# One Trainium2 core, attention into a snake MLP: transposes of two batches reordered, one MLP pass with four PSUM slots and no output matmuls

## The chip, the cores and the metric

The kernel runs on one core of one Trainium2 chip. The metric is device time in microseconds of one execution, given as the median of several runs. The program is written with an explicit order: each engine (TensorE is PE, its weight loads are PEld, VectorE is DVE, ScalarE is ACT, GpSimd is POOL, SyncE is SP) executes its instructions in the order in which the kernel's Python code emits them, and semaphores order the engines against each other.

## The reference

There are 4 batches of 8 heads with 768 positions and head size 64. The sequence is cut into chunks of 32 queries; each chunk attends to 8 memory keys, 16 keys to the left, its own 32 and 8 to the right. The attention output, laid out as 3072 tokens of 512 numbers, goes through an MLP with a "snake" activation:

```
scores = scale * q_c @ k_full.T          # k_full: 8 memory keys + local context
a      = softmax(scores)
out[:, :, chunk] = a @ v_full
x = out as (4*768, 8*64)
h = x @ w_in                             # 512 -> 2048
s = sin(alpha * h)
g = h + s * s / (alpha + 1e-9)
y = g @ w_out                            # 2048 -> 512
```

Inputs and output are float32; the kernel computes its matmuls in bfloat16 and accumulates in float32.

## The kernel before, in words

**One batch at a time, four times over.** For each batch an attention stage produces `xT`, the attention output transposed (512 features on 4x128 partitions, 768 tokens). Then a `layer` runs the first MLP matmul over 16 feature tiles `ft`: `first` issues 8 matmuls of 384 columns (L454) into a two-bank PSUM slot, ACT takes the sine (L474), one of ACT, DVE or POOL squares it (letters A, V, P of a string; L478 for ACT, L481 for the other two), and DVE's `finish` (L484) makes `gT[ft]` and frees the slot. The finish of `ft` is emitted in the next iteration, or two later when POOL squares. The number of slots in the ring `h` says how far PE may run ahead of the finishes.

**The output matmuls are a feed.** `second(i, gT)` is a generator of 6x16 matmuls of 512 columns (L497) for batch i; sub-block s copies its bank to `o_sb` on DVE if s is even (L508) and on ACT if odd (L510), and SP sends it out (L511). `feed.take(n)` puts the next n of these matmuls into PE's order at that point. So batch i's output matmuls are spread through the attention stage of batch i+1 (the tuple `shares` gives how many a step takes, half before the values, half after) and through its `layer` (`to_feed`).

**Batch 0.** `attention_first` works by head pairs. `turns(hp)` transposes keys and queries on PE (L232) into the two banks of ring `t`; `put_k` copies the keys' middle on ACT (L239) and their two edges on DVE (L245), `put_q` copies the queries on DVE (L251). `sc(hp)` issues two units of scores (mask bias L323, products L331), each followed by one exponential on ACT (L338). Then come eight units of values: `pv` is 8 matmuls (L350), followed by a reciprocal and a multiply on DVE (L356, L357); `x` is 4 transposes (L367) and an ACT copy into `xT` (L370). `warm(1)` is one matmul of 512 columns on zeros (L318), whose result is used by nobody; it takes a bank from ring `one`, as `x` does. `put_memv(0)` (L188) writes batch 0's memory values into the values tile on DVE. `ahead` issues the first half of the MLP's first three feature tiles.

**Batch 1.** POOL's `pair_up` (L220) lays two heads side by side, `turn` transposes them on PE (L229), and `put_k`/`put_q` copy as above. `put_memk(1)` (L198) writes the memory keys into the key tile on DVE.

**Batches 2 and 3.** `load_rows(b)` loads keys and queries by POOL's DMA queue into `kst` and `qst`. `cross(b)` lets SP transpose them by DMA, first eight key tiles (L159), then six query tiles (L161). It is emitted in `layer(b-1)` at `ft == 2`. SP's queue is in order too: before `cross(2)` stand the output DMAs of attention stage 1 and the eight DMAs of `send_memv(2)` (L195).

**Attention of batches 1 to 3** has 8 blocks of 96 queries. Step s issues `scores` of block s (L265, then three exponentials L278), and `values` of block s-2 (L291, reciprocal L297, multiply L298 on DVE) and `turn_x` of block s-3 (L308, DVE copy L311). The activation table of ACT is changed before and after the exponentials.

POOL's queue at the start issues, in this order: keys and queries of batch 0 (8 DMAs), memory values, V of batch 0 (two edges and eight parts), the first MLP weight (5), the second (2), keys and queries of batch 1.

Of the kernel before, what the change touches and what calls it, by code (L numbers as in the profile page):

```python
# [9 lines left out]
P = 128  # L10
# [3 lines left out]
BF = mybir.dt.bfloat16  # L14
F32 = mybir.dt.float32
ACTF = mybir.ActivationFunctionType
# [26 lines left out]
def kernel(  # L43
# [12 lines left out]
    nc = tc.nc  # L56
    B, H, S, D = q.shape
# [4 lines left out]
    HP = H // 2  # L62
# [11 lines left out]
    blk = ctx.enter_context(tc.tile_pool(name="blk", bufs=3))  # L74
# [35 lines left out]
    kTs = [consts.tile([P, HP, KW], BF, name=f"kT{i}") for i in range(2)]  # L110
# [9 lines left out]
    memk_st = consts.tile([P, 2, H * D], BF, name="memk_st")  # L120
# [42 lines left out]
    def load_qk(b, bufs, h0, h1):  # L163
        for src, dst in ((k, bufs[0]), (q, bufs[1])):
            nc.gpsimd.dma_start(
                dst[:, h0:h1].rearrange("p h r d -> p h (r d)"),
                src[b, h0:h1].rearrange("h (p r) d -> p h (r d)", p=P),
            )

    def load_v(b, parts=((0, H),)):  # L170
        vw = vws[b % 2][:].rearrange("p h j c -> p (h j) c")
        vf = v[b].rearrange("h (j t) d -> t (h j) d", t=QW)
        n = H * NJ
        if len(parts) > 1:
# [41 lines left out]


    def pair_up(src, hp):
        pr = blk.tile([P, 6, 2, D], BF, name="pr")
        nc.gpsimd.tensor_copy(  # L220
            pr[:].rearrange("p r e d -> p e r d"), src[:, 2 * hp:2 * hp + 2]
        )
        return pr

    def turn(src, hp, pr):
        t = packed(single("t"), 6, P)
        for r in range(6):
            if pr is not None:
                nc.tensor.transpose(t[:, r, :], pr[:, r].rearrange("p e d -> p (e d)"), ident[:])  # L229
            else:  # L230
                for e in range(2):
                    nc.tensor.transpose(  # L232
                        t[64 * e:64 * e + 64, r, :], src[:, 2 * hp + e, r, :], ident[:]
                    )
        return t

    def put_k(b, hp, t):
        kT = kTs[b % 2]
        nc.scalar.copy(  # L239
            kT[:, hp, 72:72 + 7 * 104].rearrange("p (s c) -> p s c", c=104)[:, :, 0:96]  # L240
            .rearrange("p s (a r) -> p s a r", r=6),
            t[:, :, 8:120].rearrange("p r (s a) -> p s a r", a=16),
        )
        for t0, c0 in ((0, 16), (120, 800)):
            nc.vector.tensor_copy(  # L245
                kT[:, hp, c0:c0 + 48].rearrange("p (a r) -> p a r", r=6),
                t[:, :, t0:t0 + 8].rearrange("p r a -> p a r"),
            )

    def put_q(b, hp, t, scalar=False):  # L250
        (nc.scalar.copy if scalar else nc.vector.tensor_copy)(  # L251
            qTs[b % 2][:, hp, :].rearrange("p (a r) -> p a r", r=6),
            t.rearrange("p r a -> p a r"),
        )
# [60 lines left out]
    def warm(n):  # L315
        z = single()
        for _ in range(n):
            nc.tensor.matmul(z, idle[:, 0:P], idle[:])  # L318
# [55 lines left out]
    def attention_first(kq, alphas, ahead):  # L374
        xT = xp.tile([P, KT, S], BF, name="xT")
        pt, xb = {}, {}

        def turns(hp):
            put_k(0, hp, turn(kq[0], hp, None))
            put_q(0, hp, turn(kq[1], hp, None))  # L380

        def sc(hp):
            for half in range(2):
                pt[hp, half] = unit_scores(hp, half)

# [12 lines left out]
        warm(2)  # L398
        turns(1)
        sc(0)  # L400
        alphas()
        sc(1)
        turns(2)
        sc(2)
        turns(3)
        put_memv(0, nc.vector, 0, H)
        sc(3)
        nc.scalar.preload_act_table(ACTF.Sin)
        send_memv(1)
        plan(big=rings["t"][0:1] + rings["big"])  # L410
        units = [(hp, half) for hp in range(HP - 1) for half in range(2)]
        pv(0, 0)
        for n in range(1, len(units)):
            pv(*units[n])
            warm(1)
            x(*units[n - 1])
            warm(1)
        pv(3, 0)
        x(2, 1)
        pv(3, 1)  # L420
        x(3, 0)
        ahead(0, 0, xT)
        ahead(1, 0, xT)
        x(3, 1)
        ahead(2, 0, xT)
        return xT
# [89 lines left out]
    kq = alloc_qk()  # L516
# [12 lines left out]
    for hp in range(1, HP):  # L529
        load_qk(0, kq, 2 * hp, 2 * hp + 2)  # L530
    nc.gpsimd.dma_start(memv_st[64:72].rearrange("n b h d -> n (b h) d"),
                        mem_v.rearrange("b h n d -> n (b h) d"))
    load_v(0, [(2 * hp, 2 * hp + 2) for hp in range(HP)])
    for kT in kTs:
        nc.vector.memset(kT[:, :, 0:16], 0.0)
        nc.vector.memset(kT[:, :, 848:856], 0.0)
# [34 lines left out]

    feed = Feed()
    xT = attention_first(kq, alphas, ahead)
    for c in range(2):
        load_w_out(c)
    kq1 = alloc_qk()
    load_qk(1, kq1, 0, H)

# [4 lines left out]
    def layer(i, xT, squares, begin, to_feed):  # L583
        gT = gTs[i % 2]
        pend = []
        fed = 0
        for ft in range(FT):
            begin(ft)
            square = squares[ft % len(squares)]
            squared, fin = first(ft, xT, gT, square, begun.pop(ft, None))  # L590
            want = to_feed * (ft + 1) // FT
            feed.take(want - fed)
            fed = want
            for due, f in [p for p in pend if p[0] <= ft]:
                f()
            pend = [p for p in pend if p[0] > ft]
            squared()
            pend.append((ft + (2 if square == "P" else 1), fin))
        for due, f in pend:
            f()  # L600
        feed.add(second(i, gT), NSUB * FT)

    def begin_0(ft):
        if ft == 3:
            plan(h=[6] + rings["big"])
        if ft == 9:
            load_v(1)

    layer(0, xT, "VPAPAAVPAAVAVPAA", begin_0, 0)
    last4 = rings["h"]  # L610
    plan(one=(last4[0], last4[0] + 1), t=(last4[1], last4[1] + 1), big=last4[1:])
    for bb in range(2):
        nc.gpsimd.dma_start(memk_st[64:72].rearrange("n b (h d) -> n b h d", d=D)[:, bb],
                            mem_k[2 + bb].rearrange("h n d -> n h d"))
    put_memk(1)
    feed.take(8)
    prs = [pair_up(kq1[n % 2], n // 2) for n in range(3)]
    for pc in range(2 * HP):
        t = turn(None, pc // 2, prs[pc])
        (put_k if pc % 2 == 0 else put_q)(1, pc // 2, t)  # L620
        if pc + 3 < 2 * HP:
            prs.append(pair_up(kq1[(pc + 3) % 2], (pc + 3) // 2))
        feed.take(2)
        if pc == 2 * HP - 2:
            nc.scalar.preload_act_table(ACTF.Exp)
    feed.take(4)
    load_rows(2)
    xT = attention(1, feed, (4, 4, 4, 3, 3, 3, 3, 3, 3, 3, 3), 2, 0)
    load_v(2)
    send_memv(2)  # L630

    for i in range(1, B):
        last = i == B - 1

        def begin(ft, i=i):
            if ft == 2 and i + 1 < B:
                cross(i + 1)

        plan(h=rings["big"])
        layer(i, xT, "AAAV", begin, feed.left() - (0 if last else 16))  # L640
        if not last:
            if i + 2 < B:
                load_rows(i + 2)
            plan(big=rings["h"])
            nc.scalar.preload_act_table(ACTF.Exp)
            xT = attention(i + 1, feed, (10, 8, 4, 4, 3, 3, 3, 3, 4, 4, 4), 2, 5 if i == B - 2 else 0)
            if i + 2 < B:
                load_v(i + 2)
                send_memv(i + 2)
# [31 lines left out]
```

## Time and profile before

| what | value |
|---|---|
| median of 5 runs | 232.55 us (230.77 to 235.52) |
| the profiled execution's own time | 233.45 us |
| span of the profile, first to last instruction | 231.7 us |
| PE busy | 216.7 us, 94% of the span |
| DVE, ACT, POOL busy | 135.9, 153.2, 81.8 us |
| largest groups on PE | L497 101.9 us x384, L454 91.9 us x512 |

The page counts a matmul busy from its issue to its modelled end, and matmuls overlap in the pipeline; so 94% is not 94% of peak, and the time that one matmul costs the queue is read from start to start: 0.2165 us for 512 columns and 0.163 us for 384 columns in the dense stages. A bracket in a timeline row says how long the engine was idle before the row and what ended that. What lies outside the span is 1.75 us.

The stages lie so in the profile: batch 0's transposes, scores and values 5.5 to 33, its MLP pass 33 to 55.5, batch 1's transposes 57.7 to 65.7, its attention 65.7 to 81.5, its MLP pass 81.5 to 107, attention of batch 2 107 to 125, its MLP pass to 156, batch 3 to 206, the last output matmuls to the end.

### The profile page before, as it was taken

Reading aid. Unit: us, or ns where it says so; the run is one execution under the profiler, and the core shown is the slowest. Engines: PE = TensorE matmul, PEld = TensorE weight load, DVE = VectorE, ACT = ScalarE, POOL = GpSimd, SP = SyncE. Lnnn points to the kernel's source line nnn. Section 1 sums busy time; section 2 is a strip of 40 time slices with the busy share of each in tenths; the row PEclk is TensorE's granted clock in tenths of the full one; section 3 lists DMA queues with packets and bytes.
Section 4 is the critical chain, followed back from the end, with each engine's and each line's share of the span. In section 5 each row is a group of like instructions: output and inputs, shape, how many; then the busy total and the mean of one; then the engine's idle time right before and its main releaser. Section 6 shows DMA issues by size and latency. Waiting matters only on the chain.

```text
span 231.7 us, 4408 instructions
## 1 busy us (share of the span) xinstructions
PE 216.7 (94%) x1701; PEld 117.2 (51%) x1701; DVE 135.9 (59%) x237; ACT 153.2 (66%) x224; POOL 81.8 (35%) x104
## 2 busy tenths in 40 slices
PE   6798689999997999999989999999999999999993
PEld 2454455654544655554555555554555555554441
DVE  5413864899927837877475476646773655652110
ACT  2264647898396679999874977789857678670111
POOL 8879502397999940688480000000000000000000
PEclk9999999999999999999999999999999999999999
DMA  5999999999999999899999945541350101102212
GB/s 81 157 141 141 199 207 207 205 184 98 38 143 120 147 142 143 104 156 177 184 148 145 73 88 97 99 130 53 88 96 31 45 3 45 45 6 91 91 45 91
DMA packets 94629, 25.96 MB, mean 112 GB/s; under 512 B 82688, under 2 KB 91536, under 8 KB 94608
## 3 DMA queue, kind: packets, MB, share of 16 engines
q0 software_dynamic: 71648, 14.82, 97.4%
q1 hardware_dynamic: 22960, 10.86, 20.7%
q8 instruction: 13, 0.21, 0.4%
q14 instruction: 8, 0.07, 0.1%
HBM read 29.67 MB, written 6.29 MB: 155 GB/s over the span
## 4 chain that ended last, share of the span: by engine, by line
PE 71%; DVE 13%; ACT 7%; issue 3%; DMA 3%; POOL 2%; DVEq 0%; ACTq 0%; POOLq 0%
PE ps L497 33%; PE ps L454 25%; DVE gT L484 5%; ACT u L474 4%; PE ps L265 3%; DMA q_bf<-in_q_dram 3%; PE ps L291 2%; DVE u L481 2%; ACT u L478 2%; PE ps L323 2%; DVE x_blk L298 1%; PE ps L308 1%; PE ps L331 1%; PE ps L229 1%; PE ps L232 1%
## 5 line engine op out<-in xcount | busy, mean ns | idle before, releaser
L497 PE MATMUL ps<-w_out_sb,gT 128*128 128x512 bf16 x384 | 101.9, 379 | 1.6 <-DVE o_sb L508 0.8
L454 PE MATMUL ps<-xT,w_in_sb 128*128 128x384 bf16 x512 | 91.9, 326 | 1.2 <-DVE gT L484 0.8
L484 DVE SCALAR_TENSOR_TENSOR gT<-u,inv_alpha,ps 128x768 bf16<-128x768 f32 x64 | 64.0, 1012 | 30.2 <-ACT u L478 27.6
L474 ACT ACTIVATE u<-ps,alpha_sb 128x768 f32<-128x768 f32 x64 | 56.9, 895 | 20.1 <-PE ps L454 20.1
L454 PEld LDWEIGHTS <-w_in_sb 128*128 128x128 bf16 x512 | 49.7, 98 | 38.9 <-issue 3.0
L497 PEld LDWEIGHTS <-gT 128*128 128x128 bf16 x384 | 34.3, 97 | 30.8 <-issue 1.6
L478 ACT ACTIVATE u<-u 128x768 f32<-128x768 f32 x44 | 37.1, 843 | 1.4
L278 ACT ACTIVATE pt<-ps,biasm 128x256 bf16<-128x256 f32 x72 | 28.7, 476 | 6.3 <-issue 2.8
L510 ACT COPY o_sb<-ps 128x512 f32<-128x512 f32 x12 | 7.0, 587 | 23.7 <-PE ps L497 23.7
L508 DVE COPY o_sb<-ps 128x512 f32<-128x512 f32 x12 | 8.2, 687 | 21.2 <-PE ps L497 21.2
L481 DVE TENSOR_TENSOR u<-u 128x768 f32<-128x768 f32 x16 | 15.2, 953 | 4.2 <-ACT u L474 4.1
L298 DVE TENSOR_TENSOR x_blk<-ps,rinv 96x512 bf16<-96x512 f32 x24 | 16.5, 687 | 1.0 <-DVE rinv L297 0.2
L139 POOL DMA_DIRECT2D kst<-in_k_dram x16 | 11.3, 704 | 12.6 <-DMA kT<-kst 11.8
L481 POOL TENSOR_TENSOR u<-u 128x768 f32<-128x768 f32 x4 | 6.4, 1597 | 18.5 <-ACT u L474 18.5
L297 DVE RECIPROCAL rinv<-ps 96x8 f32<-96x8 f32 x24 | 4.9, 203 | 13.5 <-PE ps L291 7.7
L239 ACT COPY kT<-ps 128x672 bf16<-128x672 bf16 x8 | 5.7, 718 | 10.6 <-PE ps L232 6.6
L152 POOL DMA_DIRECT2D qst<-in_q_dram x12 | 10.6, 918 | 3.7 <-DMA qT<-qst 3.7
L144 POOL DMA_DIRECT2D kst<-in_k_dram x16 | 11.8, 736 | 0.0
L291 PEld LDWEIGHTS <-pt 128*128 128x128 bf16 x192 | 9.1, 98 | 4.7 <-issue 0.8
L338 ACT ACTIVATE pt_first<-ps 128x768 bf16<-128x768 f32 x8 | 6.4, 810 | 7.6 <-PE ps L331 7.6
L318 PE MATMUL ps<-idle 128*128 128x512 bf16 x20 | 8.4, 502 | 1.6 <-DVE vw L525 1.2
L291 PE MATMUL ps<-vw,pt 128*128 128x65 bf16 x192 | 9.8, 193 | 0.0
(75 smaller groups left out, 160.6 us busy)
## 6 DMA issues: line engine op xcount, KB each, us to landing
out_dram<-o_sb SPq DMA_DIRECT2D x24, 256.0 KB
vw<-in_v_dram POOLq DMA_DIRECT2D x6, 384.0 KB, 10.4
w_out_sb<-in_moe_w_out_dram POOLq DMA_DIRECT2D x2, 1024.0 KB, 18.9
w_in_sb<-in_moe_w_in_dram POOLq DMA_DIRECT2D x3, 512.0 KB, 10.1
qst<-in_q_dram POOLq DMA_DIRECT2D x12, 128.0 KB, 6.3
kst<-in_k_dram POOLq DMA_DIRECT2D x14, 64.0 KB, 3.9
kst<-in_k_dram POOLq DMA_DIRECT2D x14, 56.0 KB, 4.0
k_bf<-in_k_dram POOLq DMA_DIRECT2D x4, 192.0 KB, 5.3
```

The source lines that it names most:

```text
L139: nc.gpsimd.dma_start(kst[r0:64, j, :].rearrange("p (h d) -> p h d", d=D), k[b, :, lo + r0:lo + 64, :].rearrange("h p d -> p h d"),)
L144: nc.gpsimd.dma_start(kst[72:72 + n, j, :].rearrange("p (h d) -> p h d", d=D), k[b, :, QW * j + 48:QW * j + 48 + n, :].rearrange("h p d -> ...
L152: nc.gpsimd.dma_start(qst[:, t, :].rearrange("p (h d) -> p h d", d=D), q[b, :, P * t:P * t + P, :].rearrange("h p d -> p h d"),)
L278: nc.scalar.activation(pt[:, 0:H * QW].rearrange("p (g e c) -> p g e c", g=2, e=4)[:, :, :, 32 * m:32 * m + 32], sc[:, :, 0:4 * QW].rearra ...
L291: nc.tensor.matmul(otv[:, e, hp, :], pt[:, QW * i:QW * i + P], vws[b % 2][:, 2 * hp + e, j, 0:D + 1],)
L298: nc.vector.tensor_tensor(out=x_blk[:].rearrange("p g e d -> p e g d"), in0=otv[0:QW, :, :, 0:D], in1=rinv[:].unsqueeze(3).to_broadcast([Q ...
L454: nc.tensor.matmul(hT[:, hf, 0:HALF], w_in_sb[:, kt, P * ft:P * ft + P], xT[:, kt, HALF * hf:HALF * hf + HALF], start=(kt == 0), stop=(kt ...
L474: nc.scalar.activation(u[:], hT[:, :, 0:HALF], ACTF.Sin, scale=alpha_sb[:, ft:ft + 1])
L478: nc.scalar.activation(u[:], u[:], ACTF.Square)
L481: eng.tensor_tensor(out=u[:], in0=u[:], in1=u[:], op=ALU.mult)
L484: nc.vector.scalar_tensor_tensor(out=gT[:, ft, :].rearrange("p (e c) -> p e c", e=2), in0=u[:], scalar=inv_alpha[:, ft:ft + 1], in1=hT[:, ...
L497: nc.tensor.matmul(o, gT[:, ft, P * s:P * s + P], w_out_sb[:, ft, :], start=(ft == 0), stop=(ft == FT - 1),)
```

## The change

For batch 0, the transposes of head pair 3 are emitted ahead of the scores of pair 2; the keys' edges are copied after the queries; V's eight part loads become six (with the two edges, eight DMAs instead of ten); the ten `warm(1)` of the values loop go. The squares of its MLP pass change from 4 V, 4 P, 8 A to 5 V, 3 P, 8 A, with no P after feature tile 8. The two small loads of memory keys move from behind this pass to ahead of it, and the first three `pair_up` of batch 1 move into it, at feature tile 14; there are four buffers for them instead of three.

For batch 1, the four key pairs are turned first, then the four query pairs, of which ACT copies every second one; the load of the exponential's table comes after all of them. The attention stage takes 52 output matmuls of batch 0 instead of 36. Its MLP pass takes none instead of 16, its ring has four slots instead of three, and its squares are 7 V and 9 A instead of 4 V and 12 A.

Ahead of the scores of batches 2 and 3 six output matmuls are taken, and the shares of the first step go from 10 to 4.

```diff
-        pr = blk.tile([P, 6, 2, D], BF, name="pr")
+        pr = blk.tile([P, 6, 2, D], BF, name="pr", bufs=4)
...
+    def put_k_edges(b, hp, t):
+        kT = kTs[b % 2]
+        for t0, c0 in ((0, 16), (120, 800)):
+            nc.vector.tensor_copy(
+                kT[:, hp, c0:c0 + 48].rearrange("p (a r) -> p a r", r=6),
+                t[:, :, t0:t0 + 8].rearrange("p r a -> p a r"),
+            )
...
         def turns(hp):
-            put_k(0, hp, turn(kq[0], hp, None))
+            tk = turn(kq[0], hp, None)
+            put_k(0, hp, tk)
             put_q(0, hp, turn(kq[1], hp, None))
+            put_k_edges(0, hp, tk)
...
         turns(2)
-        sc(2)
         turns(3)
         put_memv(0, nc.vector, 0, H)
+        sc(2)
         sc(3)
...
             pv(*units[n])
-            warm(1)
             x(*units[n - 1])
-            warm(1)
...
-    load_v(0, [(2 * hp, 2 * hp + 2) for hp in range(HP)])
+    load_v(0, ((0, 2), (2, 4), (4, 8)))
...
     load_qk(1, kq1, 0, H)
+    for bb in range(2):
+        nc.gpsimd.dma_start(memk_st[64:72]...[:, bb], mem_k[2 + bb]...)
...
+        if ft == 14:
+            prs.extend(pair_up(kq1[0], n) for n in range(3))
-    layer(0, xT, "VPAPAAVPAAVAVPAA", begin_0, 0)
+    layer(0, xT, "VAVPAPAVPAAVAVAA", begin_0, 0)
...
-    for bb in range(2):
-        nc.gpsimd.dma_start(memk_st[64:72]...[:, bb], mem_k[2 + bb]...)
     put_memk(1)
     feed.take(8)
-    prs = [pair_up(kq1[n % 2], n // 2) for n in range(3)]
     for pc in range(2 * HP):
-        t = turn(None, pc // 2, prs[pc])
-        (put_k if pc % 2 == 0 else put_q)(1, pc // 2, t)
+        hp = pc % HP
         if pc + 3 < 2 * HP:
-            prs.append(pair_up(kq1[(pc + 3) % 2], (pc + 3) // 2))
+            prs.append(pair_up(kq1[(pc + 3) // HP], (pc + 3) % HP))
+        t = turn(None, hp, prs[pc])
+        if pc < HP:
+            put_k(1, hp, t)
+            put_k_edges(1, hp, t)
+        else:
+            put_q(1, hp, t, hp % 2 == 1)
         feed.take(2)
-        if pc == 2 * HP - 2:
-            nc.scalar.preload_act_table(ACTF.Exp)
+    nc.scalar.preload_act_table(ACTF.Exp)
     feed.take(4)
     load_rows(2)
-    xT = attention(1, feed, (4, 4, 4, 3, 3, 3, 3, 3, 3, 3, 3), 2, 0)
+    xT = attention(1, feed, (8, 10, 6, 4, 4, 4, 4, 3, 3, 3, 3), 2, 0)
...
-        plan(h=rings["big"])
-        layer(i, xT, "AAAV", begin, feed.left() - (0 if last else 16))
+        if i == 1:
+            assert feed.left() == 16
+            plan(h=rings["big"] + [min(rings["one"])])
+            layer(i, xT, "VAVAVAVAAVAAVAVA", begin, 0)
+            free = rings["h"]
+            plan(one=(free[0], free[0] + 1), h=free[1:])
+        else:
+            plan(h=rings["big"])
+            layer(i, xT, "AAAV", begin, feed.left() - (0 if last else 16))
...
-            xT = attention(i + 1, feed, (10, 8, 4, 4, 3, 3, 3, 3, 4, 4, 4), 2, 5 if i == B - 2 else 0)
+            feed.take(6)
+            xT = attention(i + 1, feed, (4, 8, 4, 4, 3, 3, 3, 3, 4, 4, 4), 2, 5 if i == B - 2 else 0)
```

More of the change, by code (lines that the diff above doesn't have):

```diff
@@ L243, in put_k @@
         )
[L244 to L248, printed above, removed]
     def put_q(b, hp, t, scalar=False):
@@ L577 @@
     load_qk(1, kq1, 0, H)
+    for bb in range(2):
+        nc.gpsimd.dma_start(memk_st[64:72].rearrange("n b (h d) -> n b h d", d=D)[:, bb],
+                            mem_k[2 + bb].rearrange("h n d -> n h d"))
     gTs = [gp.tile([P, FT, S], BF, name="gT") for _ in range(2)]
@@ L601, in layer @@
         feed.add(second(i, gT), NSUB * FT)
+    prs = []
     def begin_0(ft):
@@ L607, in begin_0 @@
             load_v(1)
-    layer(0, xT, "VPAPAAVPAAVAVPAA", begin_0, 0)
+        if ft == 14:
+            prs.extend(pair_up(kq1[0], n) for n in range(3))
+    layer(0, xT, "VAVPAPAVPAAVAVAA", begin_0, 0)
     last4 = rings["h"]
     plan(one=(last4[0], last4[0] + 1), t=(last4[1], last4[1] + 1), big=last4[1:])
-    for bb in range(2):
-        nc.gpsimd.dma_start(memk_st[64:72].rearrange("n b (h d) -> n b h d", d=D)[:, bb],
-                            mem_k[2 + bb].rearrange("h n d -> n h d"))
     put_memk(1)
     feed.take(8)
-    prs = [pair_up(kq1[n % 2], n // 2) for n in range(3)]
     for pc in range(2 * HP):
-        t = turn(None, pc // 2, prs[pc])
-        (put_k if pc % 2 == 0 else put_q)(1, pc // 2, t)
+        hp = pc % HP
         if pc + 3 < 2 * HP:
-            prs.append(pair_up(kq1[(pc + 3) % 2], (pc + 3) // 2))
+            prs.append(pair_up(kq1[(pc + 3) // HP], (pc + 3) % HP))
[5 more added lines that the diff above has]
+            put_q(1, hp, t, hp % 2 == 1)
         feed.take(2)
-        if pc == 2 * HP - 2:
-            nc.scalar.preload_act_table(ACTF.Exp)
+    nc.scalar.preload_act_table(ACTF.Exp)
     feed.take(4)
     load_rows(2)
-    xT = attention(1, feed, (4, 4, 4, 3, 3, 3, 3, 3, 3, 3, 3), 2, 0)
+    xT = attention(1, feed, (8, 10, 6, 4, 4, 4, 4, 3, 3, 3, 3), 2, 0)
     load_v(2)
```

## The prediction

> **What bounds the kernel now.** First the page's busy shares and its chain by engine, then the stages one by one.
>
> ```profile
> PE 216.7 (94%) x1701; PEld 117.2 (51%) x1701; DVE 135.9 (59%) x237; ACT 153.2 (66%) x224; POOL 81.8 (35%) x104
> PE 71%; DVE 13%; ACT 7%; issue 3%; DMA 3%; POOL 2%; DVEq 0%; ACTq 0%; POOLq 0%
> ```
>
> PE carries the end, but 29% of the chain lies elsewhere. The view by windows says where (columns: window, its length, busy time and instruction count of PE, PEld, DVE, ACT, POOL, then granted clock, DMA share, GB/s):
>
> ```profile
> 23.30:26.70 3.40, 1.96 (x36) 1.20 (x36) 2.84 (x5) 2.78 (x3) 3.25 (x3) 1.00 1.32 196
> 35.00:55.50 20.50, 19.84 (x121) 11.62 (x119) 16.38 (x17) 18.37 (x23) 10.41 (x8) 1.00 1.86 184
> 65.66:81.48 15.82, 14.45 (x198) 8.30 (x198) 9.49 (x24) 11.49 (x28) 15.82 (x21) 1.00 1.65 131
> 81.48:107.00 25.52, 24.93 (x148) 13.96 (x145) 17.06 (x18) 22.68 (x28) 12.94 (x19) 1.00 1.91 140
> 125.00:156.30 31.30, 31.30 (x182) 17.22 (x182) 17.85 (x19) 24.50 (x30) 0.00 (x0) 1.00 0.80 102
> ```
>
> From 125 us on PE is full: nothing of the change helps there, and what is gained must come before. Batch 0's values are loose, both MLP passes nearly full, attention 1 has over 1 us of holes.
>
> **Batch 0 up to its MLP pass.** The chain of waits shows the values loop turning in 1.11 us:
>
> ```profile
> 27.57 0.38 PE ps L318
> 27.94 0.19 PE ps L367 x4
> 28.15 0.49 ACT xT L370
> ```
>
> ACT's copy frees the bank, a warm-up matmul takes it, the next transposes come behind. Without L318 the loop falls to DVE: L356 starts at 25.67 and 26.52 where nothing holds it, 0.85 us a unit. The start moves too. Keys of pair 3 need the bank of pair 2's keys, which the edge copies now free only after the query copy: queries of pair 2 end at 17.62, copy 0.87, edges 0.32, so keys 3 start at 18.93 (PE idles 1.4 us where it idled 0.64 and 0.63 on query copies). Queries 3 from 19.57, scores of 2 from 20.2 (1.19 us a unit, 2.37 for both), scores of 3 from 22.6; at the faster rate that PE has from 23.3 they end at 24.35. `put_memv` (1.70 us), which held the values until 25.19, is done at 23.4 and drops out. First values 24.35 instead of 25.23. Reciprocal 0.44 later, at 24.79; seventh unit normalised at 24.79+6x0.85+0.94 = 30.83; its transposes and copy (0.36+0.49, waits included 0.96) release the MLP at 31.8 instead of 33.87: **2.1 us gained**. ACT's sine table (1.28) ends near 26.6, in front of the first copy, and holds nothing. The V loads: two POOL issues of 0.72 fewer, the same bytes; the first MLP weight lands 5 to 12 us after 18.6 to 21.6, before its use, so I take 0.
>
> **Batch 0's MLP pass.** PE needs 16x1.30 = 20.8; DVE 16x0.97+5x1.0 = 20.5 (one more than before); ACT 16x0.91+8x0.75 = 20.6. Following the ring of four step by step with these durations, old squares against new, PE ends 0.3 later and the last finish 0.6 later. POOL has the pair copies done by 53, under this pass. **0.3 to 0.6 lost.** Last matmul near 53.8, last finish near 57.2 (before 58.64).
>
> **Batch 1's transposes.**
>
> ```profile
> 57.74 0.51 PE L229 MATMUL ps<-ident,pr 128*128 128x128 bf16 x6 [0.29 <-POOL pr L220]
> 59.67 0.49 PE L229 MATMUL ps<-ident,pr 128*128 128x128 bf16 x6 [0.23 <-DVE kT L245]
> 61.42 0.49 PE L229 MATMUL ps<-ident,pr 128*128 128x128 bf16 x6
> ```
>
> A pair of turns takes 1.75 us, because POOL makes each `pr` in 0.77. Three are ready beforehand and two DMA issues (1.18) leave POOL's way, so PE sets 0.77 a turn. What comes late instead is DVE: `put_memk` and the first edges stand behind the last finish, so the third keys start only at 58.15 instead of 57.1. Then, queue by queue: fourth keys 58.9, queries 59.7, 60.45, 61.35 (waits for DVE's 0.94 query copy), 62.1; six output matmuls; first scores at 63.75 (65.66 before). ACT's last query copy and table load end at 64.55, before its exponentials held anything: those begin 1.5 earlier. **1.9 gained so far.**
>
> **Attention 1.** Its steps before, from scores to scores: 1.26, 1.25, 1.49, 1.44, 1.45, 2.85, 1.45, 1.35, and 3.28 for the last three. The 2.85 holds one stall:
>
> ```profile
> 75.14 0.33 PE L308 MATMUL ps<-ident,x_blk 96*128 96x96 bf16 x4 [1.25 <-DVE o_sb L508]
> ```
>
> A sub-block's end fell ahead of a turn in the same step, and the turn waited for the bank's copy. The new shares put that end into step 2, where no turn runs. So 1.2 goes, 16x0.2165 = 3.46 come, and I add 0.3 where the next sub-block ends (ACT's copy stands behind exponentials): 15.8+3.46-1.2+0.2 = 18.2. MLP of batch 1 starts at 81.95: **the 1.9 is spent, and 0.5 more.**
>
> **Batch 1's MLP pass.** PE 20.8 instead of 24.3. DVE 16x0.97+7x1.0 = 22.5, ACT 16x0.91+9x0.75 = 21.3. DVE is the longest, but starts 3 us in and works 3 us past PE's end; the fourth slot absorbs that. Stepped through: 21.5 us of PE instead of 25.4. PE would be free at 103.45, after six output matmuls at 104.75, against 107.01: **3.9 gained in this stage, 2.2 ahead.** The last finishes end near 106 and would hold the second scores there.
>
> **What is late next: SP's transposes for batch 2.**
>
> ```profile
> 82.26 6.87 SPq L195 DMA_DIRECT2D vw<-memv_st x8
> 90.64 10.89 SPq L159 DMA_TRANSPOSE kT<-kst x8
> 101.62 7.88 SPq L161 DMA_TRANSPOSE qT<-qst x6
> ```
>
> The view of tile qT says that weight loads L265 waited for it already:
>
> ```profile
>   DMA qT<-qst: 0.4, 1
> ```
>
> So the first query tile landed near 106.9, 5.3 after its issue. The 8+6 transposes go at 1.3 each, and SP reaches them after the last output DMA of attention 1 (81.83) and `send_memv(2)`. After the change fourteen transposes still stand behind an output DMA at the end of attention 1: sub-block 4 now ends there, copied on DVE, out at 82.4. Then 6.95 for the eight loads: 89.8, not 90.64, since POOL, done with the pair copies near 60 instead of 63, issues V of batch 2 about 3 us earlier, and I expect the 1.4 us of landing wait to go. First queries land near 106.1. Scores of block 0 start there, not at 104.75; blocks 1 and 2 at 107.2 and 109.3, against 109.55 and 111.66. The later query tiles land 1.3 apart, ahead of their blocks. From here both kernels do the same: **2.4 us gained.** Bounds of this wait: if the landing wait stays, 1.6; if queries land as soon as PE is ready, 3.3, where the last finish binds.
>
> **Sum.** 2.1-0.4+0.2 = 1.9 to the first scores, -2.4 in attention 1, +3.9 in the MLP pass: 3.4. Less 1.35 for the wait for queries, plus 0.3, because the 18 output matmuls and two scores behind the pass cost 18x0.2165+2x0.28 = 4.46 by issue where 4.74 passed: 2.4. Against the profiled execution, 233.45: 231.05. The median shown is 0.9 below that execution, so 230.1 on its scale. A difference under about 1%, 2.3 us, can hardly be told from none here.
>
> **A rule that speaks to the fillers.** The same bias matmul costs twice as much early as later:
>
> ```profile
> 13.76 0.82 PE L323 MATMUL ps<-biasb,ident 128*128 128x384 bf16 x2
> 23.79 0.50 PE L323 MATMUL ps<-biasb,ident 128*128 128x384 bf16 x2
> ```
>
> The row's clock reads 1.00 in both, so I go by the durations: PE becomes fast near 23.3. The Trainium skill (TensorE: Matmul & The Clock Gate, Part 1) says the clock is halved by default, opens after about 3.4 us of busy PE and closes after an idle window as long. By it the fillers buy nothing: the new loop never idles 0.6 us, and the sum stands. By the trace opening isn't so prompt: from 10.4 to 17.2 PE is busy without a gap and stays slow. In the new loop PE has 0.41 us of issue in 0.85 (47%); nearest row 23.30:26.70, busy 58% and still fast. I take 0. Ends: 0.5 gained if it opens one window earlier; if it is closed for W us of the MLP pass, W/2 lost.
>
> **Rivals.**
> - *Clock closed into the MLP pass.* Place: L454 after 31.8; 2.6 us a feature tile instead of 1.3. Two windows by the page (6.8 us, estimate) cost 3.4: 233.5. It ends slower than before from W = 5, beyond 1% from W = 9.5; with 12, as long as PE's slow busy stretch here, 6.0 are lost: 236. For: fillers stood there, and the slow opening. Against: PE is denser ahead of the loop than in 23.3 to 26.7.
> - *Waits eat the rest.* Attention 1's stalls come back (1.2) and SP starts no earlier (0.8): 232.1; it shifts SP too, since SP hangs on this stage's end.
> - *Queries land in time.* V and memory values land early and SP waits for nothing, PE at its own pace: 3.3 to 4, so 228.9.
> - *The change does not do what it says.* Each engine follows the emitted order, so I give this nothing apart.
>
> **How the numbers follow.** Forecast 0.48 (own range 229.0 to 231.6; faster 0.30, same 0.18). Clock 0.25 (slower 0.17, same 0.08). Waits 0.12 (same 0.07, slower 0.05). In time 0.15 (faster). Sum: faster 0.45, same 0.33, slower 0.22. Range 227.8 to 235.5: it takes in the clock case up to W = 10.
>
> **What would show it.** Right: L356 every 0.85 us in the loop; first scores of batch 1 near 63.8 and no wait on POOL; no stall on L508 in attention 1, which lasts 18; L454 of batch 1 in 21.5; scores of batch 2 waiting over 1 us for qT. Wrong: L454 of batch 0 above 0.163 from start to start after 32, or the transposes L159 starting after 91.

## The result: slower by 0.8%, and the profile after

| | before | after |
|---|---|---|
| median, us | 231.70 (228.79 to 235.52, 78 runs) | 233.68 (231.04 to 236.82, 41 runs) |
| profiled execution, us | 233.45 | 234.52 |

The ratio is 1.0082, 95% interval [1.0059, 1.0106]: 1.9 us lost where 2.4 were forecast to be gained. Ratios here leave out runs more than 1.5% above the fastest of their kernel; medians are over all runs. In the kernel after, most lines of the listing stand three lower: L265 is L268, L454 is L457, L497 is L500, L508 is L511, L511 is L514.

Busy shares and the chain by engine, of after:

```profile
PE 213.7 (92%) x1691; PEld 115.6 (50%) x1691; DVE 137.5 (59%) x239; ACT 152.5 (66%) x223; POOL 79.8 (34%) x101
PE 62%; DMA 14%; DVE 11%; issue 4%; ACT 4%; SPq 2%; POOL 1%; DVEq 0%; POOLq 0%; ACTq 0%
```

PE has 3 us less to do, and the span is longer. On the chain PE fell from 71% to 62%, while DMA rose from 3% to 14%: the time went into waits for transfers. The windows by stage of after say where (batch 1's turns, its attention, its MLP pass, and the start of batch 2; columns as before):

```profile
56.30:63.56 7.26, 5.88 (x52) 3.37 (x53) 4.03 (x13) 3.63 (x6) 6.18 (x10) 1.00 3.18 122
63.56:81.69 18.13, 17.78 (x213) 9.93 (x213) 9.62 (x25) 12.64 (x28) 16.43 (x21) 1.00 1.90 153
81.69:103.30 21.61, 21.39 (x132) 12.51 (x130) 18.79 (x22) 19.11 (x23) 6.43 (x10) 1.00 2.03 105
103.30:112.71 9.41, 6.28 (x34) 2.29 (x35) 3.68 (x4) 5.81 (x11) 7.30 (x10) 0.82 1.86 152
```

Attention and MLP pass are full of PE and as long as forecast. The last stretch has 6.28 of 9.41 us, and a mean clock of 0.82. PE's timeline of after in it (a bracket is idle time before the row):

```profile
103.30 1.46 PE L500 MATMUL ps<-w_out_sb,gT 128*128 128x512 bf16 x6
106.95 0.34 PE L268 MATMUL ps<-qT,kT 64*128 64x96 bf16 x8 [2.19 <-DMA qT<-qst]
107.23 1.04 PE L500 MATMUL ps<-w_out_sb,gT 128*128 128x512 bf16 x4
109.20 0.50 PE L268 MATMUL ps<-qT,kT 64*128 64x96 bf16 x8 [0.94 <-DMA qT<-qst]
109.64 3.14 PE L500 MATMUL ps<-w_out_sb,gT 128*128 128x512 bf16 x8
112.71 0.34 PE L268 MATMUL ps<-qT,kT 64*128 64x96 bf16 x8
```

PE is through at 104.76 and then stands for query tiles twice, 3.1 us in all. Then eight output matmuls take 3.14 us instead of 1.9, since the granted clock is 0.50 from 108.8 to 112.2. Why the queries are late is in SP's timeline of after, and in its chain of waits:

```profile
82.16 0.33 SPq L514 DMA_DIRECT2D out_dram<-o_sb  x1
82.58 9.54 SPq L195 DMA_DIRECT2D vw<-memv_st  x8
92.23 10.54 SPq L159 DMA_TRANSPOSE kT<-kst  x8
102.86 8.20 SPq L161 DMA_TRANSPOSE qT<-qst  x6
```

```profile
82.16 9.21 DMA out_dram<-o_sb
...
91.44 0.69 SPq L195
...
92.23 1.31 SPq L159
```

Seven of the eight memory-value DMAs leave 0.8 apart; the eighth leaves at 91.44, just when sub-block 4's output DMA, issued at 82.16, has completed, 9.21 us later. Everything behind it on SP shifts: the transposes start at 92.23 instead of 90.64 before, although their stage starts no later. Why the eighth: in every trace SP's DMAs signal eight semaphores in turn, so the eighth DMA behind an output shares the output's semaphore, and it left only when the output had completed. The transposes themselves don't wait for V's data: in run a1 below they leave at 82.52, and V's last part lands at 93.8.

The third scores of batch 2 begin at 112.71 (before 111.66), and the last output matmul at 228.73 (before 227.68): the 1.05 us between the profiles is complete here, and nothing is added later. The other 0.9 of the medians' 2.0 belongs to no stage of these two profiles: the profiled execution of before was 1.75 above its median, that of after 0.84.

### The profile page after: what moved, and what is told of

It reads as the page before. It is cut to its first block, busy times and chain, and to the rows that moved or that the text cites. A ratio compares the mean times of both kernels' runs of the same rounds, so it can differ in the third digit from the quotient of the medians.

```text
span 232.7 us, 4389 instructions
## 1 busy us (share of the span) xinstructions
PE 213.7 (92%) x1691; PEld 115.6 (50%) x1691; DVE 137.5 (59%) x239; ACT 152.5 (66%) x223; POOL 79.8 (34%) x101
## 3 DMA queue, kind: packets, MB, share of 16 engines
q1 hardware_dynamic: 22960, 10.86, 21.6%
## 4 chain that ended last, share of the span: by engine, by line
PE 62%; DMA 14%; DVE 11%; issue 4%; ACT 4%; SPq 2%; POOL 1%; DVEq 0%; POOLq 0%; ACTq 0%
PE ps L500 31%; PE ps L457 21%; DMA out_dram<-o_sb 7%; DMA q_bf<-in_q_dram 3%; DVE gT L487 3%; DVE u L484 2%; DMA qT<-qst 2%; PE ps L268 2%; PE ps L326 2%; DMA kT<-kst 2%; PE ps L294 2%; DVE x_blk L360 2%; SPq L159 2%; DVE x_blk L301 1%; PE ps L232 1%
## 5 line engine op out<-in xcount | busy, mean ns | idle before, releaser
L500 PE MATMUL ps<-w_out_sb,gT 128*128 128x512 bf16 x384 | 100.6, 383 | 1.7 <-DVE o_sb L511 0.8
L457 PE MATMUL ps<-xT,w_in_sb 128*128 128x384 bf16 x512 | 90.1, 326 | 0.9 <-DVE gT L487 0.7
L487 DVE SCALAR_TENSOR_TENSOR gT<-u,inv_alpha,ps 128x768 bf16<-128x768 f32 x64 | 63.3, 1011 | 23.1 <-ACT u L481 20.0
L477 ACT ACTIVATE u<-ps,alpha_sb 128x768 f32<-128x768 f32 x64 | 56.8, 896 | 21.8 <-PE ps L457 21.5
L457 PEld LDWEIGHTS <-w_in_sb 128*128 128x128 bf16 x512 | 49.7, 98 | 37.8 <-issue 2.5
L500 PEld LDWEIGHTS <-gT 128*128 128x128 bf16 x384 | 34.4, 98 | 32.1 <-issue 3.3
L481 ACT ACTIVATE u<-u 128x768 f32<-128x768 f32 x41 | 34.6, 843 | 1.3
L511 DVE COPY o_sb<-ps 128x512 f32<-128x512 f32 x12 | 8.3, 688 | 27.5 <-PE ps L500 25.5
L484 DVE TENSOR_TENSOR u<-u 128x768 f32<-128x768 f32 x20 | 20.4, 1022 | 6.0 <-ACT u L477 5.9
L268 PE MATMUL ps<-qT,kT 64*128 64x96 bf16 x192 | 8.4, 208 | 3.1 <-DMA qT<-qst 3.1
L268 PEld LDWEIGHTS <-kT 64*128 64x128 bf16 x192 | 4.9, 95 | 10.7 <-issue 5.9
L254 DVE COPY qT<-ps 128x768 bf16<-128x768 bf16 x6 | 5.7, 955 | 7.1 <-PE ps L232 6.5
```

The costliest lines, as they stand in the source:

```text
L268: nc.tensor.matmul(sc[:, e, QW * hp:QW * hp + QW], kTs[b % 2][64 * e:64 * e + 64, hp, pitch * j:pitch * j + P], qTs[b % 2][64 * e:64 * e + ...
L457: nc.tensor.matmul(hT[:, hf, 0:HALF], w_in_sb[:, kt, P * ft:P * ft + P], xT[:, kt, HALF * hf:HALF * hf + HALF], start=(kt == 0), stop=(kt ...
L477: nc.scalar.activation(u[:], hT[:, :, 0:HALF], ACTF.Sin, scale=alpha_sb[:, ft:ft + 1])
L481: nc.scalar.activation(u[:], u[:], ACTF.Square)
L484: eng.tensor_tensor(out=u[:], in0=u[:], in1=u[:], op=ALU.mult)
L487: nc.vector.scalar_tensor_tensor(out=gT[:, ft, :].rearrange("p (e c) -> p e c", e=2), in0=u[:], scalar=inv_alpha[:, ft:ft + 1], in1=hT[:, ...
```

## The experiments

Medians are given as kernel / before on the same chip.

### What holds SP, and what the wait costs

Four kernels: `send_memv(2)` emitted ahead of attention 1, in after (a1) and in before (b1), so that it is off SP's way to the transposes; nine matmuls on zeros ahead of batch 2's scores, so that PE isn't idle (a2); V of batch 2 emitted later (a3).

```diff
 a1, b1
+    send_memv(2)
     xT = attention(1, feed, ...
     load_v(2)
-    send_memv(2)
 a2
             feed.take(6)
+            if i == 1:
+                warm(9)
 a3
-    load_v(2)                 # behind attention(1, ...)
+        if ft == 2 and i == 1:
+            load_v(2)         # in begin, behind cross
```

> The changed kernel, with the eight memory-value DMAs of batch 2 issued before attention 1 instead of behind it. Theory (SP's queue binds): in the changed kernel the last of these DMAs waits until 91.4 us for the landing of sub-block 4's output DMA, the key transposes start at 92.2, and scores of batch 2 wait 2.2 and 0.9 us for their queries. With the eight gone from there, the transposes start near 83, queries land near 97, and attention 2 follows at PE's own pace: third scores near 108 instead of 112.7. Time 4 to 4.7 us below the changed kernel, ratio to before 0.990 (some 229.5 us). Rival (DVE's last finishes or ACT's table load hold attention 2 as soon as queries don't): under 1.5 us gained, ratio 1.002 or more.

> The kernel before, with the same eight DMAs issued before attention 1. Theory: in the kernel before PE reaches these scores just when the queries land (wait 0.4 us in the weight load only), so there is nothing to gain: ratio 0.998 to 1.002. Rival (the transposes also disturb the kernel before, through DMA contention or a hidden wait): ratio under 0.995.

> The changed kernel, with nine unused matmuls of 512 columns on zeros (1.95 us) put into PE's order ahead of the first scores of batch 2, where PE idles 2.2 us. Theory (a second loss rides on the wait: the idle PE is throttled at 108.8 us and the next eight output matmuls take 3.14 us instead of 1.73): the clock stays open, 1.0 to 1.4 us gained, the wait for queries itself unchanged; ratio to before 1.003. Rival (the slow matmuls do not hang on the idle time, or PE's slowness is hidden by the wait): ratio 1.008 as for the changed kernel, or 1.01 if the fillers delay the scores.

> The changed kernel, with the load of V of batch 2 moved on POOL's queue from the end of attention 1 into the MLP pass of batch 1, behind the transposes' emission. Theory (sub-block 4's output DMA lands 9.2 us after its issue because V's packets stand ahead of it in the DMA engines; the outputs at 66 to 76 us landed 2.3 to 3.1 after theirs): the output lands near 85, the eighth memory-value DMA issues near 88, transposes start near 89 instead of 92.2, first scores of batch 2 near 104.8 instead of 107; 3 to 4.5 us gained, ratio to before 0.992. Rival (the landing is long by itself, or V's new place delays the transposes as much): ratio 1.005 or more.

*a1*: 229.89 / 230.25, ratio 0.9924 [0.9880, 0.9967]; the ratio rests on 5 of its 22 runs; the medians give 0.998. SP's timeline of a1, then PE's:

```profile
82.52 13.90 SPq L159 DMA_TRANSPOSE kT<-kst  x8
96.50 8.14 SPq L161 DMA_TRANSPOSE qT<-qst  x6
```

```profile
104.61 0.34 PE L268 MATMUL ps<-qT,kT 64*128 64x96 bf16 x8
106.14 0.35 PE L268 MATMUL ps<-qT,kT 64*128 64x96 bf16 x8 [0.21 <-DVE gT L487]
108.25 0.34 PE L268 MATMUL ps<-qT,kT 64*128 64x96 bf16 x8
```

The transposes leave 9.7 us earlier, no scores wait for queries, and the third scores come 4.5 us sooner. *b1*: 1.0009 [0.9982, 1.0035]. The same move gives before nothing: its scores waited 0.4 us for queries in all. So the place of `send_memv(2)` is a cost of the change only.

*a2*: 1.0122 [1.0077, 1.0168], from 6 runs; the theory's 1.003 missed. PE's timeline of a2:

```profile
104.48 2.11 PE L321 MATMUL ps<-idle 128*128 128x512 bf16 x9
...
109.04 0.34 PE L268 MATMUL ps<-qT,kT 64*128 64x96 bf16 x8 [1.07 <-DMA qT<-qst]
109.32 1.90 PE L500 MATMUL ps<-w_out_sb,gT 128*128 128x512 bf16 x8
112.11 0.34 PE L268 MATMUL ps<-qT,kT 64*128 64x96 bf16 x8 [0.89 <-DMA qT<-qst]
```

The clock stays open (1.90 for the eight again), and the third scores still begin at 112.11. The closed clock in after covered a wait for the third query tile; taken away, the wait shows.

*a3*: 1.0084 [1.0050, 1.0118], a miss. POOL's queue was idle, so V was issued at 76.1 whatever its place in the code. It repeats after, and says nothing of V. As a repeat it shows how much the last stretch varies: in its profile the clock stayed open there, and the third scores began at 110.47, not 112.71.

### V ahead of the rows; the MLP part alone

In c1 V of batch 2 is issued ahead of its keys and queries, so it is out of the way when the output DMA goes. c2 is a1 with the ten fillers back. c3 is before with the MLP part alone (four slots, the new squares, shares and six matmuls ahead); c4 is c3 with `send_memv(2)` ahead of attention 1.

```diff
 c1
+    load_v(2)
     load_rows(2)
     xT = attention(1, feed, ...
-    load_v(2)
 c2: a1, and in the values loop
+            warm(1)
             x(*units[n - 1])
+            warm(1)
 c3, from before
-    xT = attention(1, feed, (4, 4, 4, 3, 3, 3, 3, 3, 3, 3, 3), 2, 0)
+    xT = attention(1, feed, (8, 10, 6, 4, 4, 4, 4, 3, 3, 3, 3), 2, 0)
...
+        if i == 1:
+            plan(h=rings["big"] + [min(rings["one"])])
+            layer(i, xT, "VAVAVAVAAVAAVAVA", begin, 0)
...
+            feed.take(6)
```

> The changed kernel, with the load of V of batch 2 ahead of the loads of its keys and queries on POOL's queue (the run meant to move it later left it at 76.1 us, because POOL had nothing else to do: that run is a repeat of the changed kernel). Theory (V's packets delay sub-block 4's output DMA, which the eighth memory-value DMA waits for): V is in place by 75, the output issued at 82.2 lands within 4 us, the eighth DMA goes at 88.1, key transposes start near 89 instead of 92, PE waits for queries under 0.3 us; 3 to 4 us gained, ratio to before 0.993 to 0.996. Rival (the output's landing is slow for another reason, or the later rows delay the transposes): ratio 1.005 or more.

> The changed kernel with the memory-value DMAs of batch 2 issued before attention 1, and with the ten filler matmuls put back into batch 0's values loop. In three of four profiles without fillers the clock closed in that loop, near 22 to 25 us, and opened at 30 to 32; in the profile with fillers and an early clock it stayed open. Theory (the closed clock costs about what the fillers cost): fillers make the loop 1.1 us a unit instead of 0.85, 1.2 to 1.5 us in all, and the first MLP pass saves 0.9 to 1.5: ratio to before 0.991 to 0.996, as without. Rival (closing is the larger loss): ratio under 0.989. Rival (closing costs nothing, fillers do): 0.998.

> The kernel before with only the part of the change around batch 1's MLP pass: 52 output matmuls in attention 1, four slots and none in the pass, six ahead of batch 2's scores. Theory (this part makes sub-block 4's output the last ahead of the memory values, and PE early for queries that come late): attention 1 takes 2.3 us more, the pass 3.7 less, and scores of batch 2 wait over 2 us for queries; net slower, ratio 1.006 to 1.014. Rival (the loss comes from the head or the turns of batch 1): ratio 0.995 to 1.0.

> As the run with the MLP part alone, with the memory-value DMAs of batch 2 before attention 1. Theory: PE gains 3.7 in the pass and gives back 2.3 in attention 1; nothing else binds: third scores of batch 2 some 1.2 us earlier than before, ratio 0.994 to 0.996, and 1.5 to 3 us under the run without that move. Rival (late finishes and table load bind as well): no more than 0.5 us under the run without.

*c1*: 230.60 / 230.19, 1.0022 [0.9997, 1.0047], less gain than the theory's 0.993 to 0.996. SP's timeline of c1, then PE's:

```profile
83.06 0.33 SPq L514 DMA_DIRECT2D out_dram<-o_sb  x1
83.48 6.20 SPq L195 DMA_DIRECT2D vw<-memv_st  x8
89.79 10.52 SPq L159 DMA_TRANSPOSE kT<-kst  x8
```

```profile
106.06 0.34 PE L268 MATMUL ps<-qT,kT 64*128 64x96 bf16 x8 [0.41 <-DMA qT<-qst]
```

SP's order is that of after, but the eight now take 6.20 us without a hold, and the transposes start at 89.79. Some three quarters of the loss went with nothing but V's place in POOL's queue changed. By the completions that the traces record, sub-block 4's output took 4.98 us here and 9.21 in after; and the two outputs that now go with V in flight (67.09 and 70.75) took 8.59 and 7.06, where those of after (66.18 and 69.85) took 2.89 and 2.76. The slow completion moves with V: it was V's traffic, issued by POOL at 75.6 to 80.0 in after, that made the output DMA complete late.

*c3*: 235.30 / 230.19, 1.0139 [1.0048, 1.0230]: alone this part costs most, though the ratio rests on 3 of 6 runs. PE's timeline of c3 (scores are L265, output matmuls L497):

```profile
107.81 0.34 PE L265 MATMUL ps<-qT,kT 64*128 64x96 bf16 x8 [3.16 <-DMA qT<-qst]
108.09 1.04 PE L497 MATMUL ps<-w_out_sb,gT 128*128 128x512 bf16 x4
110.46 0.50 PE L265 MATMUL ps<-qT,kT 64*128 64x96 bf16 x8 [1.33 <-DMA qT<-qst]
110.89 3.60 PE L497 MATMUL ps<-w_out_sb,gT 128*128 128x512 bf16 x8
```

The same waits, longer: V is issued at 77.0 here. *c4*: 1.0000 [0.9971, 1.0028]: without the wait the loss is gone. But nothing is gained either, against the theory; PE's timeline of c4 shows why:

```profile
74.00 0.59 PE L497 MATMUL ps<-w_out_sb,gT 128*128 128x512 bf16 x2 [1.73 <-ACT o_sb L510]
```

The eight DMAs now stand on SP at 63.2 to 69.5, in front of attention 1's outputs; `o_sb` comes free late, and PE waits for the copy into it. *c2*: 0.9972 [0.9934, 1.0009], 229.54 / 230.19; with the fillers back it can't be told from a1 by the medians (0.997 and 0.998).

### The head and the turns, each alone

d1 is before with batch 0's attention part (order, edges, V loads, no fillers); d4 is d1 with the fillers kept. d2 is before with the squares, the pair copies at feature tile 14, the memory-key loads and keys-first turns. d3 is d4 with the MLP part and `send_memv(2)` ahead of attention 1.

```diff
 d1, from before
+            put_k_edges(0, hp, tk)        # behind put_q
         turns(2)
-        sc(2)
         turns(3)
         put_memv(0, nc.vector, 0, H)
+        sc(2)
...
-            warm(1)                       # both; d4 keeps them
-    load_v(0, [(2 * hp, 2 * hp + 2) for hp in range(HP)])
+    load_v(0, ((0, 2), (2, 4), (4, 8)))
 d2, from before
-    layer(0, xT, "VPAPAAVPAAVAVPAA", begin_0, 0)
+    layer(0, xT, "VAVPAPAVPAAVAVAA", begin_0, 0)
...
+        if ft == 14:
+            prs.extend(pair_up(kq1[0], n) for n in range(3))
...
+        hp = pc % HP                      # keys, then queries
```

> The kernel before with only the part of the change in batch 0's attention: transposes of pair 3 ahead of the scores of pair 2, edges behind queries, six V parts, no fillers. Theory (the prediction's 2.1 us held only against a profile whose clock opened late; with an early clock the values loop gains 1.2 to 1.5, and the clock closes in the loop without fillers): 0.3 to 1.2 us gained, ratio 0.995 to 0.999. Rival (the closed clock costs all of it): 1.0 to 1.004. Rival (the prediction's step): 0.991.

> The same part without the removal of the fillers: the ten unused matmuls stay in the values loop. Theory (fillers cost about what an open clock gives): within 0.5 us of the run without fillers, mean granted clock above 0.99 against 0.985; ratio 0.996 to 1.0. Rival (fillers are pure cost): 0.5 to 1.5 us slower than without.

> The kernel before with only the part of the change in batch 0's MLP squares and batch 1's transposes: 5 V, 3 P, 8 A, pair copies inside the pass, keys first, then queries. Theory (DVE's tail, not POOL, sets this stage: from the last matmul of the pass to the first scores of batch 1 the changed kernel took 12.2 us, the kernel before 10.6 in two profiles): 0.5 to 1.6 us lost, ratio 1.002 to 1.007. Rival (the prediction: 0.2 lost at most by the start of the scores): 0.999 to 1.001.

> The kernel before with the head part (fillers kept), the MLP part and the memory-value DMAs of batch 2 before attention 1; batch 1's transposes and batch 0's squares as before. Theory (the turns part is a loss, the others gain once SP is free): below the run with all parts, fillers and early memory values (0.997), ratio 0.992 to 0.996. Rival (the turns part is neutral): 0.996 to 0.999.

*d1*: 1.0032 [1.0006, 1.0058]; *d4*: 0.9981 [0.9946, 1.0016]. In this pair the fillers are worth some 0.5%, barely clear of the noise, and without them the head is a loss, against d1's theory; in the pair a1 and c2 no such gap shows. The windows of a1, which has no fillers, and then of d4:

```profile
21.60:25.00 3.40, 1.94 (x39) 1.59 (x40) 3.09 (x7) 2.90 (x5) 1.61 (x2) 1.00 2.08 151
25.00:28.40 3.40, 2.94 (x41) 2.57 (x40) 3.04 (x8) 1.44 (x3) 2.35 (x3) 0.50 1.33 208
```

```profile
21.60:25.00 3.40, 2.59 (x48) 1.59 (x49) 2.20 (x6) 3.23 (x5) 1.90 (x3) 1.00 1.91 169
25.00:28.40 3.40, 2.92 (x42) 2.01 (x42) 2.52 (x6) 1.49 (x4) 1.58 (x2) 1.00 1.30 210
```

After a1's window, 57% busy, the clock is closed until 31.8; after d4's, 76% busy, it stays open. The busy share alone doesn't decide, though: the kernel before had a window of 58% (23.30 to 26.70, shown in the prediction) and b1 one of 56% (18.6 to 22.0), and both stayed open after it. What the profiles do show is the link with the fillers. Without them the clock closed in the loop in five profiles of six (a1, a2, a3, c1 and d1, between 22.1 and 33.8; after is the sixth). With them it stayed open through the loop in every profile but d2's, where it was closed from 21.6 to 25.0, just after the loop began at 21.3. In d1 a V part was late as well (in a2, a3 and c1 too, by 1.5 to 1.6 us); PE's timeline of d1:

```profile
26.10 0.60 PE L353 MATMUL ps<-vw,pt_first 128*128 128x65 bf16 x8 [2.17 <-DMA vw<-in_v_dram]
```

*d2*: 1.0040 [1.0009, 1.0071], a loss by itself. *d3*: 0.9970 [0.9941, 0.9998], short of its theory; it has c4's wait for `o_sb`, 2.75 us.

### A free place for the memory values; the pair copies later

In f2 (c3) and f1 (d4 with the MLP part) the eight DMAs go ahead of batch 0's MLP pass, where SP has no outputs to send. f3 is d2 with the pair copies emitted behind the pass.

```diff
 f1, f2
     load_qk(1, kq1, 0, H)
+    send_memv(2)
...
     load_v(2)
-    send_memv(2)
 f3
-        if ft == 14:
-            prs.extend(pair_up(kq1[0], n) for n in range(3))
...
+    prs.extend(pair_up(kq1[0], n) for n in range(3))
```

> The kernel before with the head part (fillers kept), the MLP part, and the memory-value DMAs of batch 2 issued ahead of batch 0's MLP pass, where SP's queue is empty. Theory (the stall on o_sb in attention 1 was a side effect of their earlier place): no stall over 0.5 us on o_sb there, third scores of batch 2 44.7 us after the first of batch 1 (46.0 in the kernel before), 0.6 to 2 us under the run with the eight at the start of attention 1 (0.997): ratio 0.989 to 0.995. Rival (attention 1 with 52 output matmuls stalls by itself): 0.997 again.

> The kernel before with the MLP part alone and the memory-value DMAs of batch 2 ahead of batch 0's MLP pass. Theory: the part's own worth is 1.2 us of PE time, ratio 0.993 to 0.997. Rival (it is worth nothing even with SP free): 0.999 to 1.002.

> The turns part alone, with its three first pair copies on POOL behind batch 0's MLP pass as in the kernel before. Theory (POOL's copies slow DVE's squares when they run side by side): the squares of the pass all take 0.95 us and the last finish comes 0.5 us earlier than in the run with the whole turns part, but the first turn waits for its pair copy again; net within 0.5 us of that run, ratio 1.001 to 1.005. Rival (no contention): squares as slow as with it, ratio above 1.005.

*f2*: 229.12 / 230.36, 0.9952 [0.9922, 0.9982]. *f1*: 228.21 / 230.36, 0.9928 [0.9892, 0.9964], the best of all, faster than both kernels; the gains of its parts, 0.2% (d4) and 0.5% (f2), add up to it. The wait of c4 is gone; PE's timeline of f1:

```profile
74.40 0.59 PE L502 MATMUL ps<-w_out_sb,gT 128*128 128x512 bf16 x2 [0.23 <-ACT o_sb L515]
```

*f3*: 1.0046 [1.0017, 1.0075], a miss. POOL was idle, so the copies ran at 48.5 to 52.4, still inside the pass; it repeats d2.

## Why the prediction was wrong, step by step

One table holds the stages that the sum rests on (start of batch 1's first scores and of batch 2's third, us):

| kernel | first, batch 1 | third, batch 2 | between |
|---|---|---|---|
| before | 65.66 | 111.66 | 46.00 |
| forecast | 63.75 | 109.30 | 45.55 |
| after | 63.56 | 112.71 | 49.15 |
| c1 | 64.46 | 109.60 | 45.14 |
| a1 | 63.48 | 108.25 | 44.77 |
| f2 | 63.53 | 108.36 | 44.83 |

**The step that failed: "89.8, not 90.64 ... I expect the 1.4 us of landing wait to go".** The text had both DMAs in view: sub-block 4's output "out at 82.4" (82.16), and V issued about 3 us earlier (75.6). It took V's earlier issue as relief, and gave the output's completion no cost of its own. But the output goes while V's packets fill the DMA engines. It does so in the kernel before too, where V is issued at 79.30. From the view of SP's waits in before:

```profile
SPq L195 <- DMA out_dram<-o_sb: 0.6, 1, 0.6
```

There the output of 81.83 completed after 6.55 us and held the eighth memory-value DMA for these 0.6; the 1.4 was the first transpose's wait for the first memory-value DMA, which shares its semaphore. In after the output completed after 9.21 us and held the eighth for 3.4. So the 1.4 did go, but 0.6 grew to 3.4. (In c1 the eighth, 5.9 us behind the output, doesn't wait.) Why V wholly ahead of the output costs more than V 2.5 us ahead stays open. By c1 the step is worth 0.6% of the time, by a1 about 1%. The prediction's own sign of being wrong, transposes starting after 91, came with it: 92.23.

**"The later query tiles land 1.3 apart, ahead of their blocks."** They are issued 1.3 apart; the second of after completed 4.98 after its issue, and 2.2 after the first. So the step failed three times over: first scores 0.85 late (106.95 for 106.1), the second 1.15 more, the third 1.41 more. These 3.4 us turn the forecast gain of 2.4 into the 1.05 that the profiles show lost. The closed clock is in the third; in a3's profile it stayed open, and the third scores were 1.2 late.

**The fillers, "I take 0".** By d1 against d4 the value is some 1.2 us, late V parts included; by a1 against c2 it is nearly 0, so its size stays open. The bound of W/2 fits roughly: in d1 the pass ran closed for 3.8 us (29.97 to 33.81) and took 27.1 us, 1.6 more than in d4. The Trainium skill (TensorE: Matmul & The Clock Gate, Part 1) lets the clock close after an idle window of 3.4 us, and by that rule the loop would stay open. The row decides against it: in a1 a window with 1.94 us of work and no gap above 0.8 us was followed by a closed clock. The nearest row chosen, 58% "and still fast", could not tell: nearly the same share closed it in a1. In the profile of after itself the clock did stay open, and the pass ran at full speed, so the rival's place was right for other executions, not for this one.

**The head, 2.1 us.** The loop turned as forecast; DVE's timeline of after:

```profile
22.90 0.20 DVE L359 RECIPROCAL rinv<-ps 96x8 f32<-96x8 f32 x1 [1.00 <-PE ps L353]
23.75 0.19 DVE L359 RECIPROCAL rinv<-ps 96x8 f32<-96x8 f32 x1
24.58 0.20 DVE L359 RECIPROCAL rinv<-ps 96x8 f32<-96x8 f32 x1
```

That is 0.84 a unit. But most of the 2.1 was there without the change: in the profile of before PE became fast only at 23.3, in b1's at 15.2, and b1 has its first scores of batch 1 at 63.13. The profiles with before's head start their MLP pass anywhere from 27.98 (c4) to 33.13 (before itself), so one profile can't tell what the head is worth. With the fillers the head gives 0.2% (d4), which can't be told from none. The V loads, also taken at 0, held PE for 2.17 us in d1.

**Batch 0's MLP pass and the turns, "1.9 gained so far".** The total at the first scores was right (63.56), the parts were not: PE was fast from 16.6, not 23.3, and the loop began 1.9 us earlier than forecast (22.44 for 24.35), which about made up for them. From the first MLP matmul to the last finish after takes 27.2 us (29.08 to 56.30), before and b1 25.5: 1.7 lost, not 0.3 to 0.6. One square stands out, on DVE and then on POOL beside it, both of after:

```profile
50.99 2.35 DVE L484 TENSOR_TENSOR u<-u 128x768 f32<-128x768 f32 x1
```

```profile
49.40 3.12 POOL L220 COPY pr<-k_bf 128x768 bf16<-128x768 bf16 x4
```

"POOL has the pair copies done by 53, under this pass" counted them as hidden. The square takes 0.95 elsewhere; here it ends 0.8 after POOL's last copy. The Trainium skill (SBUF — State Buffer, SBUF: two separate sides) says that DVE with two SBUF inputs and a GpSimd operation that reads SBUF lock each other out. The profiles agree: in f3 it is POOL that loses, 3.92 us for the same four copies beside a square of 0.95. In f3, with its squares at full speed, the pass took 25.8, within the 0.3 to 0.6 forecast; the 27.2 of after is 1.4 more, which is the extra time of its one slow square. From first MLP matmul to first scores f3 takes 33.2 us, before 32.5, so 0.7 of f3's loss is there without a slow square; how much of the 0.4% of d2 and f3 is the lock stays open, since no run moved the copies out of the pass.

From the last finish to the first scores before takes 7.02, after 7.26; the forecast had about 6.5. PE's timeline of after:

```profile
57.19 0.49 PE L229 MATMUL ps<-ident,pr 128*128 128x128 bf16 x6 [0.98 <-DVE kT L240]
...
61.07 0.49 PE L229 MATMUL ps<-ident,pr 128*128 128x128 bf16 x6 [0.44 <-DVE qT L254]
```

No turn waits for POOL, as said. But sub-block 0's copy into `o_sb` (0.68 on DVE at 59.47) stands ahead of the first query copy, and that was left out.

**What held.** Attention 1 took 18.13 (forecast 18.2), without the stall of 1.25 and with the one of 0.23 that 0.3 was put down for. The MLP pass took 21.61 (forecast 21.5). The six output matmuls end at 104.76 (forecast 104.75). With the queries in time this part is worth 1.2 us between the two scores (a1, f2), 0.5% of the time by f2. The rival *queries land in time* describes f1, where no scores wait for queries, but f1 gained 0.7%, not the rival's 1.6%. *Waits eat the rest* named SP, at 0.8, and was nearest; neither the forecast nor a rival had SP later than before. Three slips changed little: the attention sum takes 0.2 of the 0.3 it puts down, the two rows of the bias matmul differ by 1.6 times and not twice, and the line on the weight loads' wait is of the view of tile kT.

**The parts don't add up:** alone +0.3% (d1), +0.4% (d2) and +1.4% (c3), together +0.8%. In after POOL issues V 1.4 us earlier than in c3, and the output completed after 9.21 us, in c3 after 9.99, so the shared wait is shorter there; that this is the whole difference isn't shown.

## What to carry to other kernels

When a matmul stage gets shorter, look at the queue that feeds the next one: go through every instruction in it, and ask for each DMA whose completion it needs (on SP here also that of the DMA eight places ahead) and which bulk load is in flight then. Moving eight small DMAs to a stretch where their queue was empty turned the MLP part from 1.4% lost (c3) to 0.5% gained (f2). Take the time of a stage before from more than one execution if the clock in its profile opened late, or the change is credited with what chance would have given.

## What the runs showed of the hardware

- An output DMA of 256 KB completed 6.55 (before) to 9.99 us (c3) after its issue with V's loads in flight at the end of attention 1, and 4.98 with V out of the way (c1). The eighth DMA behind it on the same queue, which shares its semaphore, left within 0.1 us of that completion in after; nothing held it in c1.
- The TensorE clock closed in a loop without a gap above 0.8 us, after a window 57% busy (a1); it stayed open after windows of 76% (d4), but also of 58% (before) and 56% (b1). It was then closed for 6.8 us (a1, until 31.8) or 10.2 us (d1, until 33.8).
- A wait can hide behind a closed clock: filling PE's idle time in a2 brought eight matmuls from 3.14 back to 1.90 us, and the next scores came only 0.6 us sooner.
- An fp32 square on DVE beside bf16 copies on POOL took 2.35 us instead of 0.95 (after), or the copies 3.92 instead of 3.12 (f3).
